# Reordering a tuned attention-plus-mixer kernel: diagonal score blocks first, key copies ahead of the cast of u, the U-product in four column groups, and products of zeros on TensorE

## Chip, cores, metric

One core of a Trainium2 chip. The metric is device time in microseconds (us) of one execution. Repeated executions of one kernel in one set of rounds lie within 1.5% of each other. "Span" is the time from the first to the last instruction of one profiled execution, about 2 us less than the device time.

## The reference

The kernel computes a local attention with a few global keys, and feeds it to a low-rank mixer and an MLP. Batch is 4, heads 8, sequence 768, head size 64.

```python
scores = q @ k.T / 8 + bias(head)          # keep: key < 8, or 0 <= row - key < 96
x   = softmax(scores) @ v                  # heads side by side: [4, 768, 512]
h   = (x.T @ U @ V).T                      # U: 768 x 32, V: 32 x 768
u   = x + h
out = u + relu(u @ w1) @ w2                # w1: 512 x 2048, w2: 2048 x 512
```

## The kernel before

Work goes by pairs of heads: four pairs to a batch, 16 in all, numbered 0 to 15. For each pair the kernel transposes q and k on TensorE (qT, kT), builds kP (the keys of the previous block, with the global keys put in front), computes eleven 128x128 score blocks for each head (five with kP, six diagonal ones with kT) in three groups called scores 0, 1 and 2, applies exp on ScalarE and multiplies masks on VectorE, forms A·V (the masked exponentials times v), normalises to x, casts x, and runs the mixer: the U-product (`mix_tmp`), the h-product (`mix_h`), the addition u = x + h, a cast of u, and the transposes of u into uT (`mix_t`). The MLP of a chunk of 512 rows (`fill`: one piece is four products of 128x512, 0.97 us) can start when its uT is there. So pairs of batch 0 have no MLP to mix in. Later pairs mix in one or two pieces at each `fill(f)`.

All instructions stand in program order on each engine; what follows is therefore also the order in which TensorE has to work. In the code NSB is 6 (row blocks of 128), R is 32, NPAIR is 4 and NP is 16. A PSUM pool is a set of buffers for what TensorE writes. The parts that matter, with cuts marked:

```python
KEEP = False
def keep_busy(bank, n):                       # products of zeros on TensorE
    for _ in range(n if KEEP else 0):
        nc.tensor.matmul(bank, zz[:, 0:P], zz, start=True, stop=True)

# previous blocks first, diagonal blocks last; scores 0, 1, 2 take 4 + 4 + 3 of them
ORDER = [(1, t) for t in range(1, NSB)] + [(0, t) for t in range(1, NSB)] + [(0, 0)]

def mix_tmp(i):                               # the U-product
    tmp_ps = ps_tp("tmp_ps", FP32, P)         # pool "tp": one buffer
    for c in range(NSB):
        nc.tensor.matmul(tmp_ps[0:R], u16[:, c], x16[:, c],
                         start=(c == 0), stop=(c == NSB - 1))
    ...
# loads: pairs 0, 1, then 2 and 3, then U, V, then w1
...
for i in range(NPAIR):                        # batch 0
    v_prev(i + 2); scores(i + 1, 0); av(i); norm(i); scores(i + 1, 1)
    if i > 0: mix_t(i - 1)
    cast_x(i); mask(i + 1, 0)
    if not last:
        transposes(i + 2, 0); mix_tmp(i); scores(i + 1, 2); transposes(i + 2, 1)
        mix_h(i, nc.vector if i == 0 else nc.gpsimd)      # cast of u on GpSimd
        ...
        mask(i + 1, 1)
        k_prev(i + 2, nc.vector if i == 0 else nc.gpsimd) # key copies, kP
    ...
    if i == 0: load(4, 2)
    if i == 1: load_w2()
    if i == 2: load(6, 2)
...
for i in range(NPAIR, NP):                    # batches 1 to 3
    v_prev(i + 2); scores(i + 1, 0); fill(f); av(i); norm(i); fill(f)
    scores(i + 1, 1); cast_x(i); fill(f); mask(i + 1, 0)
    transposes(i + 2, 0); fill(f)
    mix_tmp(i); scores(i + 1, 2); fill(f); mix_h(i, nc.gpsimd); fill(f)
    transposes(i + 2, 1); mask(i + 1, 1); k_prev(i + 2, nc.gpsimd); fill(f)
    ...
    mix_t(i)
    ...
    fill(f)
```

The softmax here doesn't subtract the row's maximum and nothing guards it: scores larger than these inputs give would overflow.

## Time and profile before

| | before |
|---|---|
| device time, median of three runs | 291.84 us (290.54 to 291.88) |
| span of the profiled run | 289.3 us |
| A·V of pair 4 starts (batch 0 is over) | 60.36 us |
| A·V of pairs 8, 12, 15 starts | 111.41, 184.03, 219.97 us |

The starts of A·V are read from the timeline of TensorE. Their distances show what one pair costs in each part of the run.

The first view is from the profile's page: busy tenths of each slice of 7.2 us, for TensorE and for the DMA engines.

```profile
PE   2564585698899999999999999988999999999994
PEclk9999999999999999999999999999999999999998
DMA  8999979960971294039120291200011200210021
```

TensorE is half idle for the first eight slices, which is batch 0. The DMA engines are nearly full in the same stretch, with a dip in the sixth slice. The clock row shows full speed throughout; the durations contradict it for batch 0, where a U-product takes 0.80 us and later 0.49 to 0.51.

The second view is the table of stretches. Its columns are: the stretch, its length, busy us and instructions of TensorE, of its weight loads, of VectorE, ScalarE and GpSimd, the granted clock, the DMA share (which comes out above 1 here and is only compared), GB/s. The first line is a pair of batch 0, the second one of batch 1, the third one of batch 2.

```profile
26.40:37.00 10.60, 6.77 (x86) 5.12 (x86) 6.15 (x10) 5.29 (x10) 2.22 (x4) 1.00 1.41 170
83.70:95.80 12.10, 11.57 (x119) 5.74 (x119) 7.33 (x12) 4.92 (x9) 2.26 (x4) 1.00 0.12 37
126.50:144.70 18.20, 18.12 (x150) 8.68 (x149) 8.95 (x15) 5.18 (x9) 4.92 (x6) 1.00 0.76 109
```

In batch 0 no engine is near full, so a chain of dependences sets the pace. In batch 2 TensorE is full. Batch 1 lies between.

The third view is the chain of waits through one pair of batch 0: start, length, and the work that the next step had to wait for.

```profile
26.47 0.61 PE sc L265 x8
...
28.98 1.07 ACT ep L270 x2
30.06 0.74 ACT x_432 L329
30.84 0.80 PE tmp_ps L336 x6
...
32.07 0.80 PE tpb L203 x12
32.89 0.77 DVE kT L215
33.66 0.10 issue
33.77 0.95 DVE x_sb L353
34.78 1.35 POOL uu L357
36.13 0.59 POOL kP L225
36.72 0.27 POOL kP L226
37.04 0.61 PE sc L265 x8
```

Read from the end: the next scores (`sc`) wait for kP; kP waits on GpSimd behind the cast of u (`uu`); that waits for u = x + h (`x_sb L353`) on VectorE, which stood behind the copy of kT. The change goes at exactly this tail.

The fourth view is what TensorE waited for (engine and line, what it waited for, us in total, times, longest). The first two lines are from batch 0 after pair 0 (26 to 58 us), the other three from 58 to 110 us, which is batch 1 with the wait that ends batch 0:

```profile
PE sc L265 <- POOL kP L226: 6.9, 2, 3.4
PE sc L265 <- DVE kP L226: 3.6, 1, 3.6
PE tmp_ps L336 <- ACT qT L211: 1.8, 4, 0.7
PE sc L265 <- POOL kP L226: 1.6, 1, 1.6
PE tpu L365 <- DVE kT L215: 0.7, 4, 0.2
```

The wait of 1.6 us for kP is the one before the first scores of batch 1, at 58.1 us.

### The profile page before, as it was taken

Reading aid. Unit: us, or ns where it says so; the run is one execution under the profiler, and the core shown is the slowest. Engines: PE = TensorE matmul, PEld = TensorE weight load, DVE = VectorE, ACT = ScalarE, POOL = GpSimd, SP = SyncE. Lnnn points to the kernel's source line nnn. Section 1 sums busy time; section 2 is a strip of 40 time slices with the busy share of each in tenths; the row PEclk is TensorE's granted clock in tenths of the full one; section 3 lists DMA queues with packets and bytes.
Section 4 is the critical chain, followed back from the end, with each engine's and each line's share of the span. In section 5 each row is a group of like instructions: output and inputs, shape, how many; then the busy total and the mean of one; then the engine's idle time right before and its main releaser. Section 6 shows DMA issues by size and latency. Waiting matters only on the chain.

```text
span 289.3 us, 5035 instructions
## 1 busy us (share of the span) xinstructions
PE 252.7 (87%) x2144; PEld 129.0 (45%) x2144; DVE 149.3 (52%) x239; ACT 104.4 (36%) x185; POOL 61.2 (21%) x80
## 2 busy tenths in 40 slices
PE   2564585698899999999999999988999999999994
PEld 1343464454444444444444444544444444444441
DVE  5646736736665665564554635666655432123221
ACT  2753552444644234533146331446431032013100
POOL 8820137102430721060200701120301100000000
PEclk9999999999999999999999999999999999999998
DMA  8999979960971294039120291200011200210021
GB/s 86 176 191 211 175 98 192 191 71 6 125 64 39 30 207 107 2 39 162 73 81 4 21 180 73 69 18 2 0 39 37 75 0 0 75 73 0 0 73 74
DMA packets 47975, 22.68 MB, mean 78 GB/s; under 512 B 31408, under 2 KB 44368, under 8 KB 47952
## 3 DMA queue, kind: packets, MB, share of 16 engines
q0 software_dynamic: 36656, 13.73, 41.1%
q1 hardware_dynamic: 11296, 8.63, 10.2%
q8 instruction: 17, 0.28, 0.4%
q14 instruction: 6, 0.05, 0.1%
HBM read 27.46 MB, written 6.29 MB: 117 GB/s over the span
## 4 chain that ended last, share of the span: by engine, by line
PE 64%; DVE 11%; ACT 10%; POOL 8%; DMA 3%; issue 2%; POOLq 0%; DVEq 0%
PE cps L399 25%; PE hps L381 21%; PE sc L265 6%; ACT ep L270 4%; DVE kT L215 4%; DMA u_111<-in_moe_U_dram 3%; DVE x_sb L353 3%; PE tmp_ps L336 3%; POOL kP L225 3%; PE h_ps L348 2%; PE ob L303 2%; PE ob L307 2%; ACT qT L211 1%; POOL qkst L98 1%; POOL uu L357 1%
## 5 line engine op out<-in xcount | busy, mean ns | idle before, releaser
L381 PE MATMUL hps<-uT,w_16_81 128*128 128x512 f16 x384 | 94.1, 383 | 0.4
L399 PE MATMUL cps<-w_16_82,htr 128*128 128x512 f16 x384 | 90.4, 380 | 0.0
L270 ACT ACTIVATE ep<-sc 128x512 f16<-128x512 f32 (+1 forms) x96 | 48.7, 560 | 90.0 <-PE sc L265 90.0
L381 PEld LDWEIGHTS <-w_16_81 128*128 128x128 f16 x384 | 34.2, 98 | 40.2 <-issue 5.1
L399 PEld LDWEIGHTS <-htr 128*128 128x128 f16 x384 | 34.4, 98 | 38.5
L386 ACT ACTIVATE htr<-hps 128x512 f16<-128x512 f32 x48 | 28.7, 598 | 62.5 <-PE hps L381 61.9
L388 DVE TENSOR_SCALAR htr<-hps 128x512 f16<-128x512 f32 x48 | 33.0, 688 | 34.6 <-PE hps L381 34.6
L357 POOL CAST uu<-x_sb 128x768 f16<-128x768 f32 x14 | 13.1, 935 | 146.9 <-DVE x_sb L353 146.9
L406 DVE TENSOR_TENSOR osb<-cps,x_sb 128x512 f32<-128x512 f32 x24 | 16.6, 690 | 34.0 <-PE cps L399 34.0
L283 DVE TENSOR_TENSOR ep<-ep,expb 128x1280 f16<-128x1280 f16 x32 | 26.2, 818 | 7.4 <-ACT ep L270 7.4
L265 PE MATMUL sc<-qT,kP 64*128 64x128 f16 x160 | 11.6, 249 | 16.2 <-POOL kP L226 8.4
L353 DVE TENSOR_TENSOR x_sb<-x_sb,h_ps 128x768 f32<-128x768 f32 x16 | 15.2, 951 | 16.6 <-PE h_ps L348 16.6
L203 PEld LDWEIGHTS <-qkst 128*64 128x64 f16 x384 | 14.6, 130 | 15.8 <-issue 10.2
L265 PEld LDWEIGHTS <-kP 64*128 64x128 f16 x160 | 5.9, 104 | 27.6 <-POOL kP L226 13.0
L319 DVE RECIPROCAL rcp<-ob 128x12 f32<-128x12 f32 x16 | 3.7, 232 | 25.2 <-PE ob L307 25.2
L225 POOL COPY kP<-kT 128x480 f16<-128x480 f16 x13 | 13.0, 1000 | 15.4 <-DVE kT L215 15.4
L320 DVE TENSOR_TENSOR x_sb<-ob,rcp 128x768 f32<-128x768 f32 x16 | 15.3, 957 | 0.6
L303 PE MATMUL ob<-vp_85,ep 128*128 128x65 f16 x160 | 15.0, 209 | 0.0
L307 PE MATMUL ob<-v_84,ep 128*128 128x65 f16 x160 | 14.9, 209 | 0.0
L203 PE MATMUL tpb<-ident_93,qkst 128*64 128x128 f16 x144 | 10.0, 314 | 5.3 <-DMA qkst<-in_q_dram 4.8
L303 PEld LDWEIGHTS <-ep 128*128 128x128 f16 x160 | 13.1, 108 | 1.6 <-issue 0.3
L307 PEld LDWEIGHTS <-ep 128*128 128x128 f16 x160 | 13.2, 109 | 0.0
(112 smaller groups left out, 204.1 us busy)
## 6 DMA issues: line engine op xcount, KB each, us to landing
out_dram<-osb SPq DMA_DIRECT2D x24, 256.0 KB, 2.0
qkst<-in_q_dram POOLq DMA_DIRECT2D x7, 384.0 KB, 5.6
qkst<-in_k_dram POOLq DMA_DIRECT2D x7, 384.0 KB, 8.3
v_84<-in_v_dram POOLq DMA_DIRECT2D x7, 384.0 KB, 11.3
w_16_81<-in_moe_w_ch_dram POOLq DMA_DIRECT2D x2, 1024.0 KB, 15.8
w_16_82<-in_moe_w_ch_dram POOLq DMA_DIRECT2D x2, 1024.0 KB, 13.4
vp_85<-v_84 SPq DMA_DIRECT2D x14, 121.9 KB, 3.0
vp_85<-v_84 SPq DMA_DIRECT2D x28, 20.3 KB, 2.5
```

Source lines behind the costliest of these rows:

```text
L203: nc.tensor.matmul(tp[64 * hi:64 * hi + 64, sb * P:(sb + 1) * P], stg[:, hi, sb], ident16, is_transpose=True, start=(sb == 0), stop=(sb == ...
L225: eng.tensor_copy(kP[:, :, G:P], kT[:, 0:NPB, G:P])
L265: nc.tensor.matmul(scs[hi][:, j * P:(j + 1) * P], lhsT, qT[r, t * P:(t + 1) * P], start=(j == 0), stop=(j == n - 1),)
L270: nc.scalar.activation(ep[:, hi, idx[0]:idx[0] + n].rearrange("p n c -> p (n c)"), scs[hi][:, 0:n * P], AF.Exp, scale=qk_scale,)
L283: nc.vector.tensor_tensor(blk, blk, eb[:, :, m:m + 1].broadcast_to((P, 2, NPB, P)), ALU.mult,)
L303: nc.tensor.matmul(ob[:, t], ep[:, hi, t - 1], vp16[:, i % VPR, hi, t - 1], start=True, stop=False,)
L307: nc.tensor.matmul(ob[:, t], ep[:, hi, NPB + t - 1], v16[:, i % VR, hi, t], start=False, stop=True,)
L353: nc.vector.tensor_tensor(xp, xp, hps[:, 0:S].rearrange("p (n c) -> p n c", n=NSB), ALU.add)
L381: nc.tensor.matmul(hh, w1_16[:, dc, jt * P:(jt + 1) * P], uT[:, dc, t0:t0 + TT], start=(dc == 0), stop=(dc == NDC - 1),)
L386: nc.scalar.activation(htr[:, jt], hh, AF.Relu)
L388: nc.vector.tensor_scalar_max(htr[:, jt], hh, 0.0)
L399: nc.tensor.matmul(cps, htr[:, jc, tt * P:(tt + 1) * P], w2_16[:, jc], start=(jc == 0), stop=(jc == NJC - 1),)
```

## The change

The intent: let the first scores need kT only (diagonal blocks first), take the cast of u from in front of the key copies in batch 0, copy kT on ScalarE, load U and V sooner, let the six matmuls of the U-product run in four column groups of the array at once (with V held four times, so that the h-product sums the four partial results), and keep TensorE's clock up in batch 0 with 31 products of zeros (eight before the first transposes, then one before each set of transposes of pairs 0 to 5 and before each group of scores of pairs 0 to 3). The main loop was reordered too. Cut to its core (left out: a second path, `DT = False`, which is dead code; the new place of `v_prev(1)`; and the order of batch 0's last pair, which changed as well):

```diff
-    KEEP = False
+    KEEP = True
-    load(2, 2)
     u16 = ...; nc.gpsimd.dma_start(u16, moe_U...)
-    v16w = cst.tile([R, S], FP16, name="v16w")
-    nc.gpsimd.dma_start(v16w, moe_V)
+    v16w = cst.tile([P, S], FP16, name="v16w")
+    nc.gpsimd.dma_start(v16w[0:R], moe_V)
+    for g in range(1, NGR):
+        nc.sync.dma_start(v16w[g * R:(g + 1) * R], v16w[0:R])
+    load(2, 2)
     load_w1()
     # kT of pairs 1 to 15
-            nc.vector.tensor_copy(ko, tv)
+            nc.scalar.activation(ko, tv, AF.Copy)
-    ORDER = [(1, t) for t in 1..5] + [(0, t) for t in 1..5] + [(0, 0)]
+    ORDER = [(0, t) for t in 1..5] + [(0, 0)] + [(1, t) for t in 1..5]
     # mask and A.V take the blocks from their new places
     # U-product
-                tmp_ps[0:R], u16[:, c], x16[:, c], start=(c == 0), stop=(c == NSB - 1),
+                tmp_ps[g * R:(g + 1) * R], u16[:, c], x16[:, c],   # g = c % 4
+                start=(c < NGR), stop=(c + NGR >= NSB), tile_position=(0, g * R),
     # batch 0
-        if i > 0: mix_t(i - 1)
-        cast_x(i); mask(i + 1, 0)
-        transposes(i + 2, 0); mix_tmp(i); scores(i + 1, 2); transposes(i + 2, 1)
-        mix_h(i, gpsimd); ...; mask(i + 1, 1); k_prev(i + 2)
+        cast_x(i); mask(i + 1, 0)
+        transposes(i + 2, 0)
+        if i > 0: mix_t(i - 1)
+        mix_tmp(i); scores(i + 1, 2); transposes(i + 2, 1)
+        k_prev(i + 2); mask(i + 1, 1); mix_h(i, vector); ...
     # batches 1 to 3
-        norm(i); fill(f)
-        scores(i + 1, 1); cast_x(i); fill(f); mask(i + 1, 0)
-        transposes(i + 2, 0); fill(f)
-        mix_tmp(i); scores(i + 1, 2); fill(f); mix_h(i); fill(f)
-        transposes(i + 2, 1); mask(i + 1, 1); k_prev(i + 2); fill(f)
-        ...; mix_t(i)
+        norm(i); transposes(i + 2, 0); fill(f)
+        scores(i + 1, 1); cast_x(i); fill(f); mask(i + 1, 0)
+        mix_tmp(i); fill(f); scores(i + 1, 2); fill(f)
+        mix_h(i); mask(i + 1, 1); transposes(i + 2, 1); k_prev(i + 2); fill(f)
+        ...; fill(f); mix_t(i)
```

More of the change, by code (lines that the diff above doesn't have):

```diff
@@ L48 @@
     D1 = D + 1
-    KEEP = False
+    KEEP = True
+    DT = False
     assert NG <= G and NL <= P - G + 1 and NPAIR == NDC
@@ L89 @@
     NP = B * NPAIR
+    NSTART = NPAIR + 2
     stage = {}
@@ L112, in load_v, with load_qk_natural @@
         )
-    def load(i0, n):
-        load_qk(i0, n)
+    def load_qk_natural(i):
+        b, hp = divmod(i, NPAIR)
+        for which, src in enumerate((q, k)):
+            stg = stp.tile([P, NSB, 2, D], FP16, name="qkn", tag="qkn", bufs=4)
+            for hi in range(2):
+                nc.gpsimd.dma_start(
+                    stg[:, :, hi],
+                    src[b, 2 * hp + hi].rearrange("(n p) d -> p n d", p=P),
+                )
+            stage[i, which] = stg
+    def load(i0, n):
+        if DT and i0 >= NSTART:
+            for j in range(n):
+                load_qk_natural(i0 + j)
+        else:
+            load_qk(i0, n)
         load_v(i0, n)
@@ L145 @@
     load(1, 1)
-    load(2, 2)
     u16 = cst.tile([P, NSB, R], FP16, name="u16")
     nc.gpsimd.dma_start(u16, moe_U.rearrange("(c p) r -> p c r", p=P))
-    v16w = cst.tile([R, S], FP16, name="v16w")
-    nc.gpsimd.dma_start(v16w, moe_V)
+    NGR = P // R
+    v16w = cst.tile([P, S], FP16, name="v16w")
[3 more added lines that the diff above has]
+    load(2, 2)
     load_w1()
@@ L188 @@
     tmps = {}
-    NSTART = NPAIR + 2
     def transposes(i, which):
@@ L194, in transposes @@
         stg = stage.pop((i, which))
+        if DT and i >= NSTART:
+            dst = qkp.tile([P, NSB, P], FP16, name="qkT", tag="qT" if which == 0 else "kT")
+            nc.sync.dma_start_transpose(dst, stg.rearrange("p n h d -> p (n h d)"))
+            if which == 0:
+                qTs[i] = dst.rearrange("p n c -> p (n c)")
+            else:
+                kTs[i] = dst
+            return
         if i < NSTART:
@@ L214, in transposes @@
             kT = qkp.tile([P, NSB, P], FP16, name="kT", tag="kT")
-            nc.vector.tensor_copy(
-                kT.rearrange("p n c -> p (n c)").rearrange("p (c n) -> p c n", n=NSB), tv,
-            )
+            ko = kT.rearrange("p n c -> p (n c)").rearrange("p (c n) -> p c n", n=NSB)
+            if i == 0:
+                nc.vector.tensor_copy(ko, tv)
+            else:
+                nc.scalar.activation(ko, tv, AF.Copy)
             kTs[i] = kT
@@ L242, in v_prev @@
                 )
-    ORDER = [(1, t) for t in range(1, NSB)] + [(0, t) for t in range(1, NSB)] + [(0, 0)]
+    ORDER = [(0, t) for t in range(1, NSB)] + [(0, 0)] + [(1, t) for t in range(1, NSB)]
     CH = [list(range(0, 4)), list(range(4, 8)), list(range(8, 11))]
@@ L250, in scores @@
             return
-        qT, kT, kP = qTs[i], kTs[i], kPs[i]
+        qT, kT, kP = qTs[i], kTs[i], kPs.get(i)
         if ci == 0:
@@ L280, in mask @@
         eb = expb[:, 2 * hp:2 * hp + 2]
-        j0, m = ((0, 2), (NPB, 1))[part]
+        j0, m = ((0, 1), (NSB, 2))[part]
         blk = ep[:, :, j0:j0 + NPB]
@@ L285, in mask @@
         )
-        if part == 1:
+        if part == 0:
             nc.vector.tensor_tensor(
-                ep[:, :, NBK - 1], ep[:, :, NBK - 1], eb[:, :, 0], ALU.mult
+                ep[:, :, NPB], ep[:, :, NPB], eb[:, :, 0], ALU.mult
             )
@@ L298, in av @@
                     nc.tensor.matmul(
-                        ob[:, 0], ep[:, hi, NBK - 1], v16[:, i % VR, hi, 0],
+                        ob[:, 0], ep[:, hi, NPB], v16[:, i % VR, hi, 0],
                         start=True, stop=True,
@@ L303, in av @@
                 nc.tensor.matmul(
-                    ob[:, t], ep[:, hi, t - 1], vp16[:, i % VPR, hi, t - 1],
+                    ob[:, t], ep[:, hi, NSB + t - 1], vp16[:, i % VPR, hi, t - 1],
                     start=True, stop=False,
@@ L307, in av @@
                 nc.tensor.matmul(
-                    ob[:, t], ep[:, hi, NPB + t - 1], v16[:, i % VR, hi, t],
+                    ob[:, t], ep[:, hi, t - 1], v16[:, i % VR, hi, t],
                     start=False, stop=True,
@@ L335, in mix_tmp @@
         for c in range(NSB):
+            g = c % NGR
             nc.tensor.matmul(
-                tmp_ps[0:R], u16[:, c], x16[:, c], start=(c == 0), stop=(c == NSB - 1),
-            )
-        tmp16 = smp.tile([R, P], FP16, name="tmp16", tag="tmp16")
-        nc.vector.tensor_copy(tmp16, tmp_ps[0:R])
+                tmp_ps[g * R:(g + 1) * R], u16[:, c], x16[:, c],
+                start=(c < NGR), stop=(c + NGR >= NSB),
+                tile_position=(0, g * R),
+            )
+        tmp16 = smp.tile([P, P], FP16, name="tmp16", tag="tmp16")
+        nc.vector.tensor_copy(tmp16, tmp_ps)
         tmps[i] = tmp16
@@ L362, in mix_t @@
         uu = u16s.pop(i)
+        if DT and i >= NPAIR:
+            nc.sync.dma_start_transpose(
+                uT[:, hp, b * S:(b + 1) * S].rearrange("p (n c) -> p n c", n=NSB),
+                uu.rearrange("p n c -> p (n c)"),
+            )
+            return
         tpu = ps_tp("tpu", FP16, S)
@@ L442 @@
         scores(i + 1, 1)
+        cast_x(i)
+        mask(i + 1, 0)
+        if i == 0:
+            v_prev(1)
+        transposes(i + 2, 0)
         if i > 0:
             mix_t(i - 1)
-        cast_x(i)
-        mask(i + 1, 0)
-        if not last:
-            transposes(i + 2, 0)
-            mix_tmp(i)
-            scores(i + 1, 2)
-            transposes(i + 2, 1)
-            mix_h(i, nc.vector if i == 0 else nc.gpsimd)
+        mix_tmp(i)
+        scores(i + 1, 2)
+        if last:
+            mix_h(i, nc.vector)
+            mask(i + 1, 1)
+            transposes(i + 2, 1)
+            k_prev(i + 2, nc.gpsimd)
+            mix_t(i)
+        else:
+            transposes(i + 2, 1)
+            k_prev(i + 2, nc.vector if i == 0 else nc.gpsimd)
+            mask(i + 1, 1)
+            mix_h(i, nc.vector)
             if i + 2 < NPAIR:
                 masks_of(i + 2)
-            if i == 0:
-                v_prev(1)
-            mask(i + 1, 1)
-            k_prev(i + 2, nc.vector if i == 0 else nc.gpsimd)
-        else:
-            mix_tmp(i)
-            scores(i + 1, 2)
-            mix_h(i, nc.vector)
-            transposes(i + 2, 0)
-            transposes(i + 2, 1)
-            mix_t(i)
-            mask(i + 1, 1)
-            k_prev(i + 2, nc.gpsimd)
         if i == 0:
@@ L489 @@
         norm(i)
+        transposes(i + 2, 0)
         fill(f)
@@ L494 @@
         mask(i + 1, 0)
-        transposes(i + 2, 0)
+        mix_tmp(i)
         fill(f)
-        mix_tmp(i)
         scores(i + 1, 2)
         fill(f)
-        mix_h(i, nc.gpsimd)
-        fill(f)
+        mix_h(i, nc.vector if DT else nc.gpsimd)
+        mask(i + 1, 1)
         transposes(i + 2, 1)
-        mask(i + 1, 1)
         k_prev(i + 2, nc.gpsimd)
@@ L507 @@
             load(i + 4, 2)
+        fill(f)
         mix_t(i)
```

## The prediction

> **What bounds the kernel before.** The table of stretches gives four parts (span 289.3 us; measured 291.84). Start and batch 0, 0 to 58.1 us: TensorE is busy 5.5 to 7.5 us in each pair of about 10.6 us, so a chain of dependences sets the pace. Batch 1, 58 to 109: pairs of 12.1 to 13.0 us with TensorE busy 11.6 to 12.1. Batch 2, 109 to 182: TensorE busy 18.1 to 18.9 us of 18.2 to 19.0, saturated. Batch 3 and the tail: nearly saturated, last 60 us pure MLP.
>
> The chain of waits in a batch-0 pair: qT/kT copies, x+h 0.95 us, cast of u on GpSimd 1.35, key copies 0.6 to 0.9, scores 0.61, then A·V, second scores, exp 1.07, cast of x 0.74, U-product 0.80, third scores, transposes 0.80, kT on DVE 0.77. TensorE idles 3.4 us per pair waiting for kP. In pair 0 the U-product also waits for the load of U, which lands at 20.06.
>
> **What the change does to it.**
> 1. Diagonal blocks first: the first four score blocks need only kT. Cast of u (1.35 on GpSimd, 0.56 on DVE) and key copies leave the chain; x+h too, mostly.
> 2. kT on ScalarE (about 0.8, as qT): frees DVE 0.96 per pair. ScalarE becomes the fullest engine in batch 0: six exps 3.1, cast 0.74, qT and kT 1.6, masks 0.9: about 6.3 us.
> 3. U and V loaded before pairs 2 and 3: U should land near 13; the 2 us wait goes.
> 4. Column groups: the U-product shrinks from 0.80 (cold) or 0.45 (warm) by an estimated 0.1 to 0.3.
> 5. 31 products of zeros, 128x512. The Trainium skill, "TensorE: Matmul & The Clock Gate", Part 1 (HAM clock gate), says TensorE runs at half clock until kept busy for some 3.4 us. The trace agrees: a U-product matmul takes 314 ns in batch 0 and 218 later; the first four MLP products take 1.82 us, later fours 0.97. I give 60% that most of batch 0 turns warm.
>
> Summed with cold durations, a batch-0 pair becomes about 8.2 us (A·V starting 15.3, 23.8, 32.2, 40), warm about 6.5. Batch 1 would start at 49 cold, 44 warm.
>
> **A cap I expect: DMA.** The DMA row is at 0.9 nearly throughout 3 to 57 us, except a gap at 36.5 to 40 because w2 is issued only at 36.9. Pairs 6 and 7's q lands at 55.9 and k at 57.9. With w2 issued near 32 the gap closes, and q lands near 52.4, k near 54.4. Pair 6's transposes come early in batch 1, so a warm batch 0 will stand there; batch 1's effective start is about 49.4 either way. Gain about 9 us.
>
> Batch 1: key copies (1.11) leave its chain; floor 11.2 to 11.5 a pair: gain 2 to 3. Batch 2: under 1. Batch 3: 1 to 2. Tail: none.
>
> **Predicted: 278.0 us**, 273.0 to 284.0. Faster by over 2%: 0.92; within: 0.06; slower: 0.02.
>
> **What would show it.** No wait of scores for kP; U-product of pair 0 waits for the cast, not DMA; batch-0 pairs 6.5 to 8.5 us; U-product matmuls near 218 ns in batch 0 if warm; w2 issued near 32; a wait for q or k of pair 6, ended near 52 to 54; batch 2 and tail unchanged.
>
> **What would make it wrong.** TensorE stays cold and the zeros (0.43 each) lie on the chain (slower, 282); copies of V or vp delayed by the full DMA rings so that pair 0's h-product or A·V stands; or DMA not binding and batch 0 warm (272).

## The result and the profile after

| | before | after |
|---|---|---|
| device time, median | 291.75 us | 282.26 us (282.06 to 284.23) |
| ratio | | 0.9699, 95% interval 0.9649 to 0.9749 |
| span | 289.3 us | 280.3 us |
| A·V of pair 4 starts | 60.36 us | 52.05 us |
| A·V of pairs 8, 12, 15 starts | 111.41, 184.03, 219.97 us | 102.98, 174.75, 210.89 us |

The median of before has a fourth run in it here. A ratio compares fast runs of both kernels in the same rounds, so it is not quite the ratio of the medians that are quoted. In a later set of rounds the same changed kernel gave 283.94 us and a ratio of 0.9795; the experiments explain part of that spread.

The starts of A·V locate the gain. At pair 4 it is 60.36 - 52.05 = 8.3 us; at pair 8 it is 8.4; at pair 12 it is 9.3; at pair 15 it is 9.1. So batch 0 gave 8.3 us, batch 1 gave 0.1, batch 2 gave 0.9, and batch 3 gave nothing.

The rows of the page (slices of 7.0 us now):

```profile
PE   7667768988989899999999999898889999999994
PEclk9688985799999999999999999999999999999999
DMA  8999999929803961191210941300001100110011
```

The DMA row is now at 9 without a dip until the eighth slice. TensorE is busier in batch 0, partly with zeros, and its clock row now shows changes.

The table of stretches, two pairs of batch 0, one of batch 1 and one of batch 2:

```profile
25.00:33.20 8.20, 6.74 (x91) 4.05 (x91) 5.21 (x10) 4.88 (x11) 0.68 (x2) 0.79 1.15 203
33.20:41.40 8.20, 5.67 (x96) 3.65 (x96) 5.75 (x11) 5.72 (x12) 3.44 (x6) 0.88 1.61 181
76.20:88.60 12.40, 11.22 (x121) 5.69 (x122) 6.14 (x10) 5.40 (x9) 2.71 (x4) 1.00 0.09 27
119.30:137.30 18.00, 17.93 (x153) 8.88 (x154) 7.52 (x12) 5.40 (x9) 2.29 (x4) 1.00 0.72 106
```

From A·V to A·V, pairs 1 and 2 take 8.2 and 7.6 us (7.6 and 7.6 in the repeat) instead of 10.6. In batch 1 TensorE has less to do than before (11.22 instead of 11.57 us), yet the pair is no shorter: it idles 1.2 us instead of 0.5. Over the whole of batch 1, from A·V of pair 4 to A·V of pair 8, it is busy 46.2 of 50.9 us, and was busy 47.9 of 51.1 before: 1.8 us less work, and 1.6 us more idle time. The chain through a pair of batch 0 shows the new links:

```profile
34.93 1.08 ACT ep L300 x2
36.03 0.83 DVE ep L313
36.86 0.20 DVE ep L317
37.06 0.48 DVE uT L408
37.58 0.29 PE tmp_ps L367 x6
37.87 0.32 PE sc L202
38.19 0.32 PE sc L295 x6
38.51 0.87 ACT ep L300 x2
39.44 0.71 issue
40.15 0.96 DVE x_sb L386
41.15 0.22 PE ob L328
```

The key copies and the cast of u are gone from it. Three things are new. The U-product (`tmp_ps`) waits for the copy of uT, which stands behind the mask products (`ep`) on VectorE, because both its own result and the transposes of u use the single buffer of one PSUM pool. A product of zeros (`sc L202`) lies on the chain. And x + h (`x_sb L386`) has not left it: A·V (`ob`) now waits for it, because the h-product and A·V share the single buffer of another pool. The waits of TensorE say the same (the first two lines are from 25 to 50 us, the other two from 58 to 110 us; the last is one of three alike there):

```profile
PE tmp_ps L367 <- DVE uT L408: 2.8, 3, 1.5
PE ob L328 <- DVE x_sb L386: 2.4, 3, 1.4
PE tpu L404 <- POOL uu L390: 1.0, 4, 0.3
PE tmp_ps L367 <- ACT x_1247 L359: 0.9, 1, 0.9
```

### The profile page after: what moved, and what is told of

Read it like the earlier page. It is cut to its first block, busy times and chain, and to the rows that moved or that the text cites. A ratio compares the mean times of both kernels' runs of the same rounds, so it can differ in the third digit from the quotient of the medians.

```text
span 280.3 us, 5103 instructions
## 1 busy us (share of the span) xinstructions
PE 252.4 (90%) x2175; PEld 125.5 (45%) x2175; DVE 134.5 (48%) x226; ACT 116.8 (42%) x200; POOL 57.1 (20%) x78
## 4 chain that ended last, share of the span: by engine, by line
PE 71%; ACT 11%; DVE 8%; POOL 4%; DMA 2%; issue 2%; POOLq 0%; DVEq 0%; ACTq 0%
PE hps L420 26%; PE cps L438 25%; ACT ep L300 7%; PE sc L295 5%; DVE x_sb L386 4%; POOL uu L390 3%; PE tp L231 2%; PE tpu L404 2%; DMA qkst<-in_q_dram 2%; PE ob L333 2%; PE ob L337 2%; PE h_ps L381 2%; PE tmp_ps L367 1%; DVE ep L313 1%; PE sc L202 1%
## 5 line engine op out<-in xcount | busy, mean ns | idle before, releaser
L420 PE MATMUL hps<-uT,w_16_81 128*128 128x512 f16 x384 | 92.7, 382 | 0.4 <-ACT htr L425 0.4
L390 POOL CAST uu<-x_sb 128x768 f16<-128x768 f32 x12 | 15.1, 1260 | 133.4 <-DVE x_sb L386 133.4
L313 DVE TENSOR_TENSOR ep<-ep,expb 128x1280 f16<-128x1280 f16 x32 | 26.3, 821 | 18.4 <-ACT ep L300 18.4
L386 DVE TENSOR_TENSOR x_sb<-x_sb,h_ps 128x768 f32<-128x768 f32 x16 | 15.2, 952 | 11.9 <-PE h_ps L381 11.9
L231 PEld LDWEIGHTS <-qkst 128*64 128x64 f16 x384 | 13.1, 120 | 8.0 <-issue 3.0
L333 PE MATMUL ob<-vp_85,ep 128*128 128x65 f16 x160 | 13.5, 200 | 1.5 <-DVE ep L313 1.5
L333 PEld LDWEIGHTS <-ep 128*128 128x128 f16 x160 | 11.8, 102 | 5.5 <-issue 2.6
L408 DVE COPY uT<-tpu 128x768 f16<-128x768 f16 x16 | 8.9, 556 | 11.1 <-PE tpu L404 11.1
L295 PE MATMUL sc<-qT,kT 64*128 64x128 f16 x192 | 11.8, 233 | 1.8 <-DVE kT L245 1.2
L337 PE MATMUL ob<-v_84,ep 128*128 128x65 f16 x160 | 13.4, 200 | 0.0
L255 POOL COPY kP<-kT 128x480 f16<-128x480 f16 x13 | 7.7, 593 | 26.1 <-ACT kT L247 26.1
L239 ACT ACTIVATE qT<-tp 128x768 f16<-128x768 f16 x10 | 8.1, 811 | 10.7 <-PE tp L231 10.7
L110 POOL DMA_DIRECT2D v_84<-in_v_dram x9 | 12.3, 1368 | 0.0
## 6 DMA issues: line engine op xcount, KB each, us to landing
v_84<-in_v_dram POOLq DMA_DIRECT2D x7, 384.0 KB, 11.5
```

Source lines behind the costliest of these rows:

```text
L231: nc.tensor.matmul(tp[64 * hi:64 * hi + 64, sb * P:(sb + 1) * P], stg[:, hi, sb], ident16, is_transpose=True, start=(sb == 0), stop=(sb == ...
L295: nc.tensor.matmul(scs[hi][:, j * P:(j + 1) * P], lhsT, qT[r, t * P:(t + 1) * P], start=(j == 0), stop=(j == n - 1),)
L313: nc.vector.tensor_tensor(blk, blk, eb[:, :, m:m + 1].broadcast_to((P, 2, NPB, P)), ALU.mult,)
L333: nc.tensor.matmul(ob[:, t], ep[:, hi, NSB + t - 1], vp16[:, i % VPR, hi, t - 1], start=True, stop=False,)
L337: nc.tensor.matmul(ob[:, t], ep[:, hi, t - 1], v16[:, i % VR, hi, t], start=False, stop=True,)
L386: nc.vector.tensor_tensor(xp, xp, hps[:, 0:S].rearrange("p (n c) -> p n c", n=NSB), ALU.add)
```

## Experiments

All kernels gave correct results. The repeat of the changed kernel came out above what was expected of it (281 to 283 us). Differences of about 1% between sets of rounds are therefore not settled by the device time alone; where they matter below, the starts of A·V in the profiles carry the reading.

| kernel | median us | ratio to before |
|---|---|---|
| changed kernel, first rounds / repeated | 282.26 / 283.94 | 0.9699 / 0.9795 |
| a: no zeros | 282.24 | 0.9713 |
| c: previous blocks first | 286.87 | 0.9851 |
| d: one column group | 286.21 | 0.9852 |
| h: MLP pieces moved | 280.08 | 0.9645 |
| i: uT first | 283.80 | 0.9775 |
| j0: pairs 6 and 7 ahead of w2 | 281.50 | 0.9697 |
| j: i and j0 together | 278.32 | 0.9593 |
| k: cast of u ahead of key copies | 284.94 | 0.9804 |
| g: main loop of before | 275.25 | 0.9489 |
| l: j without zeros | 279.37 | 0.9610 |
| m: i, j0 and MLP pieces moved | 272.69 | 0.9373 |

### The parts of the change, undone one at a time

**a, no zeros.**

```diff
-    KEEP = True
+    KEEP = False
```

> The changed kernel without the 31 products of zeros. Theory 1 (the zeros keep TensorE at full clock for part of batch 0 and this shortens the chain): all U-product matmuls of batch 0 are slow (near 314 ns), batch 1 starts 1 to 2.5 us later than 49.8, time 283.5 to 285. Rival (the zeros lie on the chain and cost what they win, or only the front of the DMA counts): time within 0.7 us of 282.3.

Measured: 282.24 us, ratio 0.9713 (0.9656 to 0.9771), not told apart from the changed kernel. A·V of pair 4 started at 51.0, earlier than the 52.05 with zeros, but the next pair took 15.1 us instead of 12.95 (14.35 in the repeat of the changed kernel), 0.7 of it waiting for q of pair 6. The U-products of pairs 0 to 2 took 0.40 us, that of pair 3 0.29, which is the fast value, so TensorE reached full clock late even without zeros. With zeros, three of the four took 0.29 us in the first profile. So the zeros raise the clock in stretches, and they take 0.38 to 0.64 us each; no net effect on the time shows. Expecting every U-product to be slow was wrong.

**c, previous blocks first again.**

```diff
-    ORDER = diagonal blocks, then previous blocks
+    ORDER = previous blocks, then diagonal blocks   # mask and A.V to match
```

> The changed kernel with the order of score blocks of before (previous-block scores first, so the first scores need kP). Theory (in batch 0 the key copies are then again between kT and the first scores): the wait for kP is back, about 1 us in each of pairs 2 to 4 and 0.5 in pair 1; batch 1 has slack for it; time 285.5 to 287. Rival (order is not what shortened batch 0, the cast of u behind the key copies is): time within 1 us of 282.3.

Measured: 286.87 us. TensorE's largest wait in batch 0 is the one foretold (columns: engine and line, what it waited for, us in total, times, longest):

```profile
PE sc L295 <- POOL kP L256: 3.1, 3, 1.5
```

A·V of pair 4 started at 54.70, 2.7 us later than in the changed kernel. So the block order takes about 3 us of waiting out of batch 0, a part of the 8.3 us, and the wait that the theory foretold is there. That "batch 1 has slack for it" did not hold: from A·V of pair 4 to A·V of pair 15 run c takes 161.3 us, the changed kernel 158.8. Where these further 2.4 us come from was not traced.

**d, one column group.**

```diff
-                tmp_ps[g * R:(g + 1) * R], ..., tile_position=(0, g * R)   # four groups
+                tmp_ps[0:R], u16[:, c], x16[:, c], start=(c == 0), stop=(c == NSB - 1)
```

> The changed kernel with the U-product in one column group and V held once. Theory: U-product 0.49 us instead of 0.29 warm in all 16 pairs, TensorE-bound parts pay 0.15 to 0.2 each, batch 0 up to 0.4 each, less 0.5 us for the wait on the copies of V in pair 0: time 284 to 285.5. Rival (hidden under other waits): within 0.7 us of 282.3.

Measured: 286.21 us, slightly above the range; its ratio, 0.9852 (0.9783 to 0.9921), is not clear of that of the repeat. The pair-to-pair distance in batch 1 is 12.68 us instead of 12.37, and in batch 2 18.4 instead of 18.2 (means of three). The six matmuls take 0.29 us instead of 0.49 at full clock, and 0.40 instead of 0.80 at half clock. By the medians the groups are worth 2 to 4 us over 16 pairs, about what was expected or a little more. The Trainium skill, "TensorE: Matmul & The Clock Gate", Part 3 (Packing small matmuls), says that matmuls in different column groups run at the same time; the trace agrees, with factors of 1.7 and 2.0 for these six matmuls.

**k, cast of u ahead of the key copies.**

```diff
-            k_prev(i + 2, ...); mask(i + 1, 1); mix_h(i, nc.vector); masks_of(...)
+            mix_h(i, nc.vector if i == 0 else nc.gpsimd); masks_of(...)
+            mask(i + 1, 1); k_prev(i + 2, ...)
```

> The changed kernel with, in the batch-0 loop, the cast of u (on GpSimd again) and the h-product's addition ahead of the mask and the key copies, as before. Theory (key copies ahead of the cast are worth about 1 us in each of pairs 1 and 2, since the second scores need kP): a wait of scores for kP of 0.5 to 1 us in these pairs; A.V of pair 3 starts near 42.5 to 43.5 instead of 41.2 to 41.9. The time may move less, as pair 6 waits for its q. Rival (diagonal blocks first already hide it): A.V of pair 3 as in the changed kernel.

Measured: A·V of pairs 1, 2 and 3 at 23.27, 33.51 and 43.08, so pairs 1 and 2 took 10.2 and 9.6 us, against 8.2 and 7.6 in the changed kernel. The waits for kP itself were 0.7 us in two waits, the longer 0.4; in addition A·V waited 2.2 us for the mask product, which now stood behind the addition u = x + h. So the order matters by about 2 us in each of these two pairs, and more through the mask than through kP. Pair 0 was shorter than in the changed kernel, so that A·V of pair 3 came 1.9 us later than there (1.2 later than in its repeat). The device time, 284.94 us, has a ratio of 0.9804, against 0.9795 in the repeat, and settles nothing.

### Where the gain of batches 1 to 3 went

**h, one MLP piece moved.**

```diff
         norm(i); transposes(i + 2, 0)
-        fill(f)
         scores(i + 1, 1); cast_x(i)
         fill(f)
         mask(i + 1, 0)
+        fill(f)
         mix_tmp(i)
```

> The changed kernel with one MLP piece of the main loop moved from before the second scores to before the U-product. Theory (batch 1 gained nothing because TensorE now waits 0.93 us per pair for exp and cast of x ahead of the U-product, with only one MLP piece of 0.97 to cover 1.07 + 0.74): this wait goes, pairs of batch 1 fall from 12.4 to about 11.5, batch 3 likewise; time 277 to 280. Rival (batch 1 is limited by TensorE's own work): within 0.7 us of 282.3.

Measured: 280.08 us, at the edge of the range, and a ratio (0.9584 to 0.9705) that is not clear of the 0.9699 of the changed kernel's first rounds; but the pairs of batch 1 fell from 12.37 to 11.78, and the wait ahead of the U-product from 0.93 to at most 0.4 us. The profiled run also stood 1.6 us for q of pair 6 (see the cap below). The place to see why is TensorE's timeline of the changed kernel between scores 1 and the U-product (start, length, instructions; in brackets the idle time before and what ended it):

```profile
79.68 0.28 PE L295 MATMUL sc<-qT,kP 64*128 64x128 f16 x4
79.89 1.04 PE L438 MATMUL cps<-w_16_82,htr 128*128 128x512 f16 x4
81.86 0.29 PE L367 MATMUL tmp_ps<-x_1247,u_106 128*32 128x128 f16 x6 [0.93 <-ACT x_1247 L359]
```

After scores 1, ScalarE needs 1.07 us for exp and 0.74 for the cast of x before the U-product can go. TensorE has one piece of 0.97 us to work on, then idles 0.93.

**g, the main loop of before, all else of the change kept.**

```diff
-        norm(i); transposes(i + 2, 0); fill(f); scores(i + 1, 1); cast_x(i); fill(f)
-        mask(i + 1, 0); mix_tmp(i); fill(f); ...
+        norm(i); fill(f); scores(i + 1, 1); cast_x(i); fill(f)
+        mask(i + 1, 0); transposes(i + 2, 0); fill(f); mix_tmp(i); ...
```

> The changed kernel with the main loop (batches 1 to 3) of before, all else kept. To be read by the profile's pair-to-pair distances in batch 1 (12.37 us in the changed kernel, 12.6 in the one without column groups), as the times of the changed kernel differ by 1% between calls. Theory (the new order of the main loop traded the wait for kP, which the block order had removed already, for a wait for the cast of x): pairs of 11.5 to 12.1 us, so faster than the changed kernel. Rival (the new order was needed to drop the kP wait): pairs of 12.5 or more.

Measured: 275.25 us, ratio 0.9489 (0.9451 to 0.9526), 2% to 3% faster than the changed kernel. Pairs of batch 1: 11.76 and 11.54 us. The same place in its timeline:

```profile
78.26 0.28 PE L295 MATMUL sc<-qT,kP 64*128 64x128 f16 x4
78.47 1.04 PE L438 MATMUL cps<-w,htr 128*128 128x512 f16 x4
79.43 0.53 PE L231 MATMUL tp<-ident,qkst 128*64 128x128 f16 x12
79.89 1.04 PE L438 MATMUL cps<-w,htr 128*128 128x512 f16 x4
81.13 0.29 PE L367 MATMUL tmp_ps<-x,u 128*32 128x128 f16 x6 [0.20 <-ACT qT L239]
```

Here two pieces and twelve transposes cover exp and cast, and 0.20 us of idle time is left. The starts of A·V give the sum against the changed kernel's profile: 1.9 us in batch 1 (51.47 to 100.46 is 48.99, against 50.93), 1.3 in batch 2, 2.2 in the three distances of batch 3, 0.6 each before pair 4 and after pair 15, together 6.7, as the spans say (280.3 and 273.6). So the other edits of the change had earned this gain in batches 1 to 3, and the reordering of the main loop in the same change gave it away. Run g also shows what the gain consists of: against the kernel before, batch 1 is 2.1 us shorter, of which 1.2 are less work on TensorE (46.7 us busy instead of 47.9; the U-product alone takes 0.2 us less in each pair) and 0.8 less idle time. The wait ahead of the U-product is as it was before, 1.8 us in four.

### The cap by loads

Batch 0 can be shortened further, since the U-product waits 2.8 us for uT in pairs 1 to 3. The prediction said that loads would cap the gain: q and k of pair 6 come last, behind w2. Two edits, alone and together, test it.

```diff
 # i: uT first
         norm(i); scores(i + 1, 1)
+        if i > 0: mix_t(i - 1)
         cast_x(i); mask(i + 1, 0); ...; transposes(i + 2, 0)
-        if i > 0: mix_t(i - 1)
         mix_tmp(i)
 # j0: pairs 6 and 7 ahead of w2
-        if i == 1: load_w2()
-        if i == 2: load(6, 2)
+        if i == 1: load(6, 2)
+        if i == 2: load_w2()
```

The changed kernel unaltered, beside them:

> The changed kernel unaltered, as the reference on this chip for the three runs beside it: 281 to 283 us, ratio to before 0.966 to 0.974; q of pair 6 lands near 53.

i alone:

> The changed kernel with the transposes of u of the last pair and their copy to uT moved ahead of the mask product in the batch-0 loop, so that the U-product no longer waits for that copy (2.8 us in pairs 1 to 3). Theory (loads cap batch 0: q of pair 6 lands near 53 whatever batch 0 does): A.V of pair 4 starts 1 to 2.5 us earlier, the transposes of pair 6 then wait for q for 1 to 2.5 us, and the time stays within 0.8 us of the unaltered one. Rival (no cap): 1.5 to 2.5 us faster.

j0 alone:

> The changed kernel with the load of pairs 6 and 7 issued ahead of w2. q of pair 6 lands near 40 to 42 instead of 53, w2 near 57, well ahead of its use near 76. Theory: as only 0.2 us of waiting for q shows in the changed kernel, the time stays within 0.8 us of the unaltered one. If it gains over 1 us, the cap binds already in a way the waits do not show.

j, both:

> Both of the edits beside it. Theory of the cap: now the gain of the first edit comes through, 1.3 to 2.5 us faster than the unaltered and than either edit alone; no wait for q of pair 6. Rival (no cap): the same as the first edit alone.

| | median us | A·V of pair 4 | A·V of pair 5 | q of pair 6 lands |
|---|---|---|---|---|
| unaltered, repeated | 283.94 | 51.96 | 66.31 | 54.7 |
| i | 283.80 | 50.05 | 68.25 | 55.1 |
| j0 | 281.50 | 51.99 | 64.38 | 40.5 |
| j | 278.32 | 48.01 | 61.02 | 40.9 |

Landing times are the issue's start plus the time to landing in the DMA view, for example 41.69 + 13.0 for the unaltered kernel. Edit i moved A·V of pair 4 forward by 1.9 us and gained nothing; its timeline shows why (the profiled execution was the slowest of its four, 285.28 us):

```profile
55.14 0.85 PE L231 MATMUL tp<-ident,qkst 128*64 128x128 f16 x12 [4.13 <-DMA qkst<-in_q_dram]
55.93 1.89 PE L420 MATMUL hps<-uT,w 128*128 128x512 f16 x4
```

TensorE stood 4.13 us for q of pair 6, more than the 1 to 2.5 foretold, and the MLP piece after it ran at half speed (1.89 us instead of 1.04; the one before the wait did so too, as it does in the changed kernel). With the loads turned round, the same edit is worth 281.50 - 278.32 = 3.2 us. The cap is shown. Both edits together gain 5.6 us over the unaltered kernel, where 1.3 to 2.5 were foretold; the excess was not taken apart. j0 alone was expected within 0.8 us and gained 2.4: the repeated unaltered run waited 1.6 us for q, where the first profile had shown 0.2. So the changed kernel sits on the edge of the cap. Its two profiled runs differ by 1.2 us in span, and they part in the pair that holds this wait (A·V of pair 5 at 65.00 and 66.31, level at pair 4): there the difference is how late q lands. That this explains all of the spread of 1.7 us between the medians was not shown, and the chip may have differed.

The time of those loads in the DMA view (KB counted as fp16, us from issue to landing), for the changed kernel and for j:

```profile
qkst<-in_q_dram POOLq DMA_DIRECT2D x1, 384.0 KB, 12.4
```

```profile
qkst<-in_q_dram POOLq DMA_DIRECT2D x1, 384.0 KB, 7.5
```

The same 384 KB take 12.4 us when issued behind w2 and 7.5 behind pairs 4 and 5.

**l, j without zeros.** Does only the cap hide what the zeros win?

> The version without the cap (uT first and pairs 6 and 7 ahead of w2, 278.3 us) without the products of zeros. Theory (the zeros cost on the chain what their clock wins, whether or not loads cap): 277.5 to 279.3. Rival (only the cap hid what they win): 280 to 282.5, with slow U-product matmuls (314 ns) all through batch 0.

Measured: 279.37 us, between the two ranges, ratio 0.9610 (0.9595 to 0.9625), against 0.9593 (0.9560 to 0.9626) for j in another set of rounds. If the zeros win anything, it is about 1 us, and these runs don't resolve it. The U-products of pairs 0 and 1 took 0.40 us and those of pairs 2 and 3 took 0.29: here TensorE reached its full clock in batch 0 without zeros, one pair sooner than in run a.

**m, the edits joined.** j, with the MLP pieces of the main loop moved: the one of h, and the last `fill(f)` of a pair from after to before `mix_t`.

```diff
 # j, h, and
         ...; fill(f)
+        fill(f)
         mix_t(i)
         ...
-        fill(f)
```

> Three edits together: uT first, pairs 6 and 7 ahead of w2, and the MLP pieces of the main loop moved to cover the exp and cast of x and the cast of u. If their gains add (3 to 5.6 for the first two, 2.2 for the third): 275 to 277 us, ratio to before 0.948 to 0.956, pairs of batch 1 near 11.5. If they overlap: 278.

Measured: 272.69 us, ratio 0.9373 (0.9353 to 0.9393), below the range: 6.3% faster than the kernel before. The gains more than add, and the second moved piece also covers the cast of u, a wait of 0.3 us a pair that had not been counted. Pairs of batch 1 take 11.67 and 11.36 us.

## Why the prediction was right or wrong

The measured 282.26 us lies inside the predicted range of 273 to 284, and "faster by over 2%" held. The middle, 278.0, was 4.3 us too low; most of that lies in batches 1 and 3 (point 6).

1. **Batch 0, right about kP and nearly in size, but in part by luck.** Predicted: pairs of about 8.2 us cold, batch 1 starting at 49, a gain of about 9. Measured: pairs of 8.2 and 7.6, the first scores of batch 1 at 49.83, a gain of 8.3. The waits for kP did go. But 8.2 us was the sum for a cold TensorE, and most U-products ran at full clock; and that x + h would mostly leave the chain was wrong. In place of kP TensorE waited 2.8 us for uT, which the prediction did not have, and 2.4 us for x + h. So the agreement of the size is partly luck: a faster clock and two waits that were not counted worked against each other, and how far they balance was not measured. Run c shows the part of the block order (about 3 us of waits), run k that of the order of cast, mask and key copies. kT on ScalarE was not undone alone; what it is worth stays open. ScalarE did become fuller in pair 0 (6.33 of 7.9 us), but not the fullest engine in the next two stretches (4.88 and 5.72 of 8.2 us, TensorE 6.74 and 5.67, VectorE 5.21 and 5.75).
2. **"The 2 us wait goes" (U and V loaded early): true and worth nothing.** U landed at 13.2. But the U-product of pair 0 started at 20.65, against 20.06 before: it now waited 1.1 us for the cast of x. Here two waits ended almost together, and removing one did not move the step.
3. **"An estimated 0.1 to 0.3" for column groups: right at full clock, too small at half clock.** It is 0.20 and 0.40, and run d puts 2 to 4 us on the whole.
4. **"60% that most of batch 0 turns warm": about half came true, and it was immaterial.** The U-products of pairs 0 to 3 took 0.29, 0.29, 0.29 and 0.40 us (0.40, 0.29, 0.29 and 0.34 in the repeat), where run a without zeros has one fast one of four. The MLP's first piece still took 1.89 us. The clock record can't decide it: the row gives 1.00, 0.79, 0.88 and 0.50 for the four stretches from 17.1 to 51.3 us, but from 15.5 to 50 us it gives 0.80 with zeros and 0.96 without (run a), against what the durations say. Without zeros the time is the same within the noise (run a), and with the cap gone the medians differ by 1 us, which is not resolved (run l). The listed danger, that zeros lie on the chain, is visible in the chain.
5. **The cap: right.** q of pair 6 was predicted for 52.4 and landed at 53.4, and 54.7 in the repeat, 2.3 us off; k was predicted for 54.4 and landed at 55.4. The 2x2 of i and j0 shows that it binds.
6. **"Batch 1: key copies (1.11) leave its chain; floor 11.2 to 11.5 a pair: gain 2 to 3" and "Batch 3: 1 to 2": the step that failed.** Measured: batch 1 gave 0.1 us and batch 3 nothing. Two terms were wrong. First, the key copies did lie in the chain of batch 1 and did leave it, but TensorE hardly stood for them: inside batch 1 of the kernel before, the idle time ahead of the scores with kP adds up to 0.4 us. It stood 1.8 us for qT ahead of the U-product and 0.7 for the copy of kT. So most of the 1.11 us a pair was already covered by MLP pieces, and taking the copies away could win little by itself. Second, the same change moved the transposes of q and one MLP piece away from between scores 1 and the U-product, where they covered exp and cast. The prediction checked that the old wait would vanish, and did not lay the new order against the chain of exp and cast: 1.07 + 0.74 us, covered by 0.97. The wait ahead of the U-product grew from 1.8 us in four to 0.93 us in each pair, and swallowed what less work on TensorE had won. Pairs of 11.4 to 11.8 us, near the predicted floor, were reached in runs g and m. With the old main loop, all else kept, batch 1 is 2.1 us and batch 3 2.0 us shorter than before (run g): 275.25 us, below the prediction's 278.

## What to carry to other kernels

When a change takes a wait off the chain and also reorders the loop, go through the new order once more and ask, for each engine that has to work in program order, what now covers each producer chain; a reordering made to help one wait can uncover another of the same length. Check too that the engine that sets the pace really stands for the link that is removed: a link can lie in the chain of waits and still be covered. Where loads and compute both run near full, find the transfer that lands last for the next stage and move it ahead of bulk that is needed later; without that, shortening the compute only lengthens a wait. Products of zeros to hold a clock won nothing here that could be measured, and some of them lay on the chain.

## What the Trainium skill lacked or had wrong

- "TensorE: Matmul & The Clock Gate", section "Why this matters for your kernels", advises against idle gaps of over about 3 us between bursts of matmuls. Keeping to this alone was not sufficient here: from 17 us to the end of batch 0 of the changed kernel the longest wait of TensorE was 1.5 us, and in two stretches it was busy 5.67 and 6.74 of 8.2 us by the profile's count; still six transposes of u took 0.51 us at 35.6 us and 0.82 at 28.5, 44.3 and 49.1. The page gives no density of work that holds the clock.
- The same page, Part 1, warns that clock records in a trace can be unreliable. In the trace of before the row reads 1.00 in batch 0, while a matmul of the U-product took 314 ns there and 218 ns later; in run a it reads 0.96 from 15.5 to 50 us, while three of four U-products were slow. Durations of one and the same matmul are the safer gauge.
- The same page, Part 3, gives speedups for matmuls of 512 columns. For six matmuls of 128 columns by 32 rows of output in four groups, the runs show 0.49 to 0.29 us at full clock and 0.80 to 0.40 at half clock.
- "DMA: Bandwidth & Descriptors", "Anatomy of one DMA", models a transfer issued by GpSimd as about 2.0 us plus bytes over bandwidth. With the DMA engines full, q of pair 6 (384 KB, issued by GpSimd) took 12.4 us to land; the three copies of V (48 KB each, issued by SyncE) took 6.4 to 7.9. No page tells how to reckon a landing behind a queue that is full; reading off the order and the landings of before was good to about 1 us for q and k of pair 6 in the first profile, and to 2.3 us for q in the repeat.
